# Swin window attention, forward and backward: turning P and dS of a quad by a DMA transpose instead of on TensorE

## The chip, the cores and the metric

The kernel runs on one core of one Trainium2 chip. The metric is the device time of one execution in microseconds. Seven executions of the kernel before took 2029.27 us in the median (2012.38 to 2056.46). The profiled execution took 2029.27 us itself; its span in the profile is 2027.5 us.

## The reference

Attention within windows of 8 x 8 tokens over an image of 256 x 256 tokens of 384 channels, and the gradients of the loss with respect to x and to both weights:

```
xw  = x in windows of 64 tokens              # 1024 windows
qkv = xw @ wqkv                              # q, k, v: 384 channels each
p   = softmax(q k^T * 384 ** -0.5)           # 64 x 64 in each window
out = (p v) @ wo, back in image order
out_1, out_2, out_3 = gradients of x, wqkv, wo for grad_out
```

Everything comes in and goes out in bfloat16.

## The kernel before, in words

The weights are multiplied with each other once at the start (A, B and their transposes), so that per window only products of x and of the gradient with 384 x 384 matrices are left. Two windows, one above the other in the image, make a tile of 128 token rows; four such tiles make a quad. There are 128 quads. `load` brings x (`xq`, from SP's queue) and the incoming gradient (`dq`, from POOL's queue) of a quad, four transfers each. `load_turn` transposes both by DMA on SP's queue, twelve blocks of 128 x 128 each (`dT`, `xT`).

The main loop is a software pipeline over quads, written by hand (L312 to L348 and L363 to L371): in one step, quad C (the oldest) has the second half of its attention products, quad B its scores, softmax and the first half of its attention products, quad A its projections. Ahead of the step, SP issues the transposes for the quad after A, and then the four x loads for the one after that. On POOL, the gradient loads stand between the stores of two steps. The instructions of each engine run in the order in which the program writes them; a step is, on TensorE:

- `scores` of B (tile `sd`), then `uv` of B (eight products of x with B and A^T), with B's softmax on VectorE and ScalarE beside them (`soft`, steps 0 to 5)
- `project(A, 0)`: the gradient's projections (`dT`), evicted by ScalarE to `yz`
- one group of the weight gradient's sums (`filler`, tile `pg`)
- `attend(C, (2, 3))`: the attention products of C's tiles 2 and 3, and after them `turn(B)`
- `project(A, 1)`: x's projections (`xT`) to `yz`; then `to_tokens` has SP transpose `yz` to `tok`, 24 blocks
- one more group of the weight gradient's sums
- `attend(B, (0, 1))`: the attention products of B's tiles 0 and 1

What `turn` works on: `ps` holds, for each tile of a quad and each of its two windows (index w), the softmax P and the score gradient dS stacked over the 128 partitions, 64 columns wide. P is written by ScalarE (L206), dS by VectorE (L218), in `soft` steps 3 and 5. `turn` makes the transposes of these blocks: eight products of `ps` with an identity matrix (L234) into a PSUM tile `pt` from the ring of eight, one VectorE copy (L237) to `PS` in bfloat16. `attend` reads `PS` through `turned` as the weights of its products into `pu`, `po` and `pd` (L256), and `ps` itself in `token_part` (L260). The results go through ScalarE (L265) to `sb` and out by POOL's stores (L246), and through VectorE to `Uq` and `Wq`.

Of the kernel before, what the change touches and what calls it, by code (L numbers as in the profile page):

```python
# [9 lines left out]
ALU = mybir.AluOpType  # L10
AX = mybir.AxisListType
BF16 = mybir.dt.bfloat16
F32 = mybir.dt.float32

P = 128
WIN = 8
WT = WIN * WIN
# [5 lines left out]
def kernel(  # L23
# [88 lines left out]
    def load(st):  # L112
        bp, t0 = st["at"]
        st["xq"] = xq = grp.tile([P, QUAD, C], BF16, tag="xq", name="xq", bufs=2 * GQ + 4)
        st["dq"] = dq = qp.tile([P, QUAD, C], BF16, tag="dq", name="dq", bufs=6)
        for t in range(QUAD):
            nc.sync.dma_start(out=xq[:, t, :], in_=dram_tile(x, bp, t0 + t))
            nc.gpsimd.dma_start(out=dq[:, t, :], in_=dram_tile(grad_out, bp, t0 + t))  # L118
# [62 lines left out]
    def soft(st, step):  # L181
        sd = st["sd"]
        if step == 0:
            st["mx"] = mx = sm.tile([P, QUAD], F32, tag="mx", name="mx")
            for w, h in ((0, HI), (1, LO)):
                nc.vector.tensor_reduce(out=mx[h, :], in_=sd[h, :, w, :], axis=AX.X, op=ALU.max)
        elif step == 1:
            mx = st["mx"]
            st["sh"] = sh = sm.tile([P, QUAD, WT], F32, tag="sh", name="sh")
            for w, h, o in ((0, HI, LO), (1, LO, HI)):  # L190
                nc.vector.tensor_tensor(out=sh[o, :, :], in0=sd[h, :, w, :], in1=over_k(mx[h, :], WT),
                                        op=ALU.subtract)
        elif step == 2:
            st["ex"] = ex = sm.tile([P, QUAD, WT], F32, tag="ex", name="ex")
            nc.scalar.activation(out=ex[:], in_=st["sh"][:], func=ACT.Exp)
        elif step == 3:
            ex = st["ex"]
            rs = sm.tile([P, QUAD], F32, tag="rs")
            nc.vector.tensor_reduce(out=rs[:], in_=ex[:], axis=AX.X, op=ALU.add)
            ri = sm.tile([P, QUAD], F32, tag="ri")  # L200
            nc.vector.reciprocal(out=ri[:], in_=rs[:])
            st["Pb"] = Pb = qp.tile([P, QUAD, WT], BF16, tag="Pb", name="Pb")
            nc.vector.tensor_tensor(out=Pb[:], in0=ex[:], in1=over_k(ri[:]), op=ALU.mult)  # L203
            st["ps"] = ps = qp.tile([P, 2, QUAD, WT], BF16, tag="ps", name="ps")
            for w, h in ((0, LO), (1, HI)):
                nc.scalar.copy(out=ps[h, w, :, :], in_=Pb[h, :, :])  # L206
        elif step == 4:
            st["pr"] = pr = sm.tile([P, QUAD, WT], F32, tag="pr", name="pr")
            for w, h in ((0, LO), (1, HI)):
                nc.vector.tensor_tensor(out=pr[h, :, :], in0=sd[h, :, w, :], in1=st["Pb"][h, :, :], op=ALU.mult)  # L210
            st["D"] = D = sm.tile([P, QUAD], F32, tag="D", name="D")
            nc.vector.tensor_reduce(out=D[:], in_=pr[:], axis=AX.X, op=ALU.add)
        else:
            pd = sm.tile([P, QUAD, WT], F32, tag="pd")
            nc.vector.tensor_tensor(out=pd[:], in0=st["Pb"][:], in1=over_k(st["D"][:]), op=ALU.mult)
            ps = st["ps"]
            for w, h, o in ((0, LO, HI), (1, HI, LO)):
                nc.vector.tensor_tensor(out=ps[o, w, :, :], in0=st["pr"][h, :, :], in1=pd[h, :, :], op=ALU.subtract)  # L218

    def uv(st, t, part):  # L220
        if t == 0 and part == 0:
# [6 lines left out]
        cp(out=dst[:, t, :], in_=pj[:])  # L228

    def turn(st):  # L230
        pt = ring.tile([P, QUAD, 2, WT], F32, tag="r", name="pt")
        for t in range(QUAD):
            for w, h in ((0, LO), (1, HI)):
                nc.tensor.matmul(pt[h, t, :, :].rearrange("p s k -> p (s k)"), lhsT=st["ps"][:, w, t, :],  # L234
                                 rhs=ident[:], start=True, stop=True)
        st["PS"] = dst = qp.tile([P, QUAD, 2, WT], BF16, tag="PS", name="PS")
        nc.vector.tensor_copy(out=dst[:], in_=pt[:])  # L237

    def turned(st, n, t, h):
        if n in ("PT", "ST"):  # L240
# [4 lines left out]
        for h, w in ((LO, 1), (HI, 0)):  # L245
            nc.gpsimd.dma_start(out=dram_tile(dst, bp, t)[WIN * w:WIN * (w + 1)], in_=src[h, :])  # L246

    def attend(st, pair, after=None):
        bp, t0 = st["at"]
        if pair[0] == 0:  # L250
            st["Uq"] = grp.tile([P, QUAD, C], BF16, tag="Uq", name="Uq")
            st["Wq"] = grp.tile([P, QUAD, C], BF16, tag="Wq", name="Wq")
        def both(straight, crossed):
            for h, o, (dst, lhs, rhs, begin, done) in ((LO, LO, straight), (LO, HI, crossed), (HI, LO, crossed),
                                                       (HI, HI, straight)):
                nc.tensor.matmul(dst[o, :], lhsT=turned(st, lhs, t, h), rhs=st[rhs][h, t, :], start=begin, stop=done)  # L256

        def token_part(t, pd, first):
            for w, o in ((0, HI), (1, LO)):
                nc.tensor.matmul(pd[o, :], lhsT=st["ps"][:, w, t, :], rhs=st["tok"][:, :, t, w, :], start=first,  # L260
                                 stop=not first)

        def keep(name, eng, dst, t, src):
            sb = ob.tile([P, C], BF16, tag=name)
            ENG[EV[eng][t]](out=sb[:], in_=src[:])  # L265
            stores.append((dst, sb, bp, t0 + t))

        stores = []
        for t in pair:
            first = t == pair[0]  # L270
            po, pu = [ring.tile([P, C], F32, tag="r", name=n) for n in ("po", "pu")]
            if first:
                pd = ring.tile([P, C], F32, tag="r", name="pd")
                token_part(t, pd, True)
            both((pu, "ST", "xq", True, True), (po, "PT", "uq", True, True))
            keep("o", "o", out_0, t, po)
            ENG[EV["U"][t]](out=st["Uq"][:, t, :], in_=pu[:])  # L277
            pw = ring.tile([P, C], F32, tag="r", name="pw")
            if not first:
                pd = ring.tile([P, C], F32, tag="r", name="pd")  # L280
            both((pw, "Pb", "dq", True, True), (pd, "ST", "vq", not first, first))
            ENG[EV["W"][t]](out=st["Wq"][:, t, :], in_=pw[:])  # L282
            if not first:
                token_part(t, pd, False)
            keep("d", "d", out_1, t, pd)
        for s in stores:
            store(*s)
        if after is not None:
            turn(after)

    fill = []

# [11 lines left out]
    def filler(n):  # L304
        while n and fill:
            try:
                next(fill[0])
                n -= 1
            except StopIteration:
                fill.pop(0)  # L310

    def step(c, b, a):  # L312


        def on(st):
            return (lambda f, *r: f(st, *r)) if st is not None else (lambda f, *r: None)
        C_, B, A = on(c), on(b), on(a)
        B(scores)
        B(soft, 0)
        B(uv, 0, 0)  # L320
        B(uv, 0, 1)
        B(soft, 1)
        B(uv, 1, 0)
        B(uv, 1, 1)
        B(soft, 2)
        B(soft, 3)
        B(uv, 2, 0)
        B(uv, 2, 1)
        for t in range(QUAD):
            A(grad_turn, t)  # L330
        B(uv, 3, 0)
        B(uv, 3, 1)
        B(soft, 4)
        for mo in range(CK):
            A(project, 0, mo)
        B(soft, 5)
        filler(1)
        if c is not None:
            attend(c, (2, 3), b)
        else:  # L340
            B(turn)
        split[0] = True
        for mo in range(CK):
            A(project, 1, mo)
        A(to_tokens)
        filler(1)
        split[0] = ALL
        B(attend, (0, 1))  # L348
# [7 lines left out]
    with tc.manual_schedule(engines=MANUAL):  # L356
        for i in range(min(AHEAD, n)):
            load(sts[i])
            if i < AHEAD - 1:
                load_turn(sts[i])  # L360
        held = []
        get = lambda i: sts[i] if 0 <= i < n else None
        for i in range(-1, n + 1):  # L363
            if AHEAD - 1 <= i + AHEAD - 1 < n:
                load_turn(sts[i + AHEAD - 1])
            if AHEAD <= i + AHEAD < n:
                load(sts[i + AHEAD])
            step(get(i - 1), get(i), get(i + 1))
            if i > 0:
                held.append(sts[i - 1])  # L370
                sts[i - 1] = None  # L371
            if held and (len(held) == GQ or i == n):
                fill.append(gf_group(held))
                held = []
        split[0] = False
        filler(1 << 30)
# [60 lines left out]
```

## Time and profile before

| What | Value |
|---|---|
| Median of seven runs | 2029.27 us (2012.38 to 2056.46) |
| Profiled execution: own time, span | 2029.27 us, 2027.5 us |
| Granted TensorE clock | 0.999 |
| TensorE busy | 1995.4 us, 98% |
| VectorE, ScalarE, POOL busy | 1396.9, 1441.7, 1418.4 us |
| One step of the loop in mid-run (`sd` to `sd`) | 15.38 us |
| L234, `turn`'s products | 1024 of 219 ns |
| L237, `turn`'s copy | 128 of 677 ns |
| dT, xT, tok: issue on SP, median | 2.24, 2.80, 5.06 us |
| dT, xT, tok: issue to landing, median | 6.0, 6.5, 9.4 us |

Busy times are of one execution. Matmuls overlap in TensorE's pipeline, so that the durations of single products add up to more than the time they hold. SP's "duration" of a DMA is the time that SP needs to issue it; its landing comes later, and other engines wait for the landing. The DMA shares count the time that packets are under way on 16 engines; packets of different queues overlap, so that shares can add up to over 100%.

### The profile page before, as it was taken

How to read it: one execution, taken by the hardware profiler on the slowest of the kernel's cores; microseconds unless marked ns; L12 is line 12 of the kernel's file. 1: busy time of each engine (PE TensorE's matmuls, PEld its weight loads, DVE VectorE, ACT ScalarE, POOL GpSimd, SP SyncE). 2: the span in 40 equal slices, each digit the busy share in tenths (PEclk: the TensorE clock that was granted, in tenths of full speed). 3: DMA queues.
4: the chain of work that ended last, by engine and by line, in shares of the span. 5: the costliest groups of instructions: out<-in, count | busy, mean ns of one | idle time of the engine just before them, and what ended most of it. 6: DMA issues, size and time to landing. Idle time of an engine off the chain costs nothing.

```text
span 2027.5 us, 54709 instructions
## 1 busy us (share of the span) xinstructions
PE 1995.4 (98%) x20442; PEld 1222.4 (60%) x20442; DVE 1396.9 (69%) x3107; ACT 1441.7 (71%) x3213; POOL 1418.4 (70%) x2566
## 2 busy tenths in 40 slices
PE   8999999999999999999999999999999999999998
PEld 4565566555566666666666666666666666666665
DVE  5766676666676677677677767767767776776775
ACT  5776777666677777777777777777777777777773
POOL 4766776766777777777776777777777677777764
PEclk9999999999999999999999999999999999999999
DMA  9999999999999999999999999999999999999993
GB/s 212 221 210 204 203 196 207 195 194 187 199 209 206 211 205 209 203 206 208 207 208 206 212 197 214 203 209 209 205 210 203 202 212 208 206 204 210 202 185 79
DMA packets 997195, 409.27 MB, mean 202 GB/s; under 512 B 880705, under 2 KB 971585, under 8 KB 996929
## 3 DMA queue, kind: packets, MB, share of 16 engines
q1 hardware_dynamic: 873648, 253.80, 76.5%
q0 software_dynamic: 122880, 151.68, 30.6%
q8 instruction: 160, 2.62, 0.6%
q14 instruction: 107, 0.87, 0.1%
q10 hardware_dynamic: 400, 0.29, 0.0%
HBM read 101.84 MB, written 101.84 MB: 100 GB/s over the span
## 4 chain that ended last, share of the span: by engine, by line
PE 89%; DMA 5%; ACT 2%; POOL 2%; issue 1%; DVE 1%; ACTq 0%; POOLq 0%
PE pj L146 33%; PE pg L146 12%; PE pj L144 11%; PE pg L144 11%; PE pd L260 6%; PE pu L256 5%; PE sd L146 5%; PE pw L256 4%; DMA out_dram<-sb 3%; PE pt L234 2%; DMA tok<-yz 1%; POOL out_dram L246 1%; DMA dq<-in_grad_out_dram 1%; PE pd L256 1%; ACT uq L228 0%
## 5 line engine op out<-in xcount | busy, mean ns | idle before, releaser
L246 POOL DMA_DIRECT2D out_dram<-sb x2048 | 1145.7, 567 | 539.6 <-ACT sb L265 198.2
L265 ACT CAST sb<-po 128x384 bf16<-128x384 f32 x512 | 250.7, 490 | 289.0 <-PE pu L256 160.3
L301 DVE TENSOR_TENSOR GF_acc<-pg,GF_acc 128x384 f32<-128x384 f32 x258 | 143.9, 558 | 430.4 <-PE pg L144 292.1
L146 PEld LDWEIGHTS <-xT 128*128 128x128 bf16 x3072 | 292.2, 98 | 189.1 <-issue 7.8
L146 PE MATMUL pj<-AT_sb,xT 128*128 128x384 bf16 x1536 | 334.2, 327 | 5.4 <-ACT sb L265 5.2
L146 PE MATMUL pj<-B_sb,xT 128*128 128x384 bf16 x1536 | 333.9, 326 | 0.0
L118 POOL DMA_DIRECT2D dq<-in_grad_out_dram x512 | 273.8, 548 | 49.0 <-issue 14.1
L277 DVE CAST Uq<-pu 128x384 bf16<-128x384 f32 x512 | 282.7, 552 | 18.9 <-PE pu L256 12.1
L228 ACT CAST uq<-pj 128x384 bf16<-128x384 f32 x512 | 248.1, 485 | 56.5 <-PE pj L146 52.4
L282 DVE CAST Wq<-pw 128x384 bf16<-128x384 f32 x512 | 279.8, 547 | 0.0
L265 ACT CAST sb<-pd 128x384 bf16<-128x384 f32 x512 | 254.2, 496 | 35.1 <-DMA out_dram<-sb 28.9
L144 PE MATMUL pj<-xT,A_sb 128*64 128x512 bf16 x2304 | 273.4, 379 | 0.0
L146 PE MATMUL pj<-dT,BT_sb 128*128 128x512 bf16 x1152 | 269.5, 379 | 0.0
L228 ACT CAST vq<-pj 128x384 bf16<-128x384 f32 x512 | 250.5, 489 | 1.9
L144 PEld LDWEIGHTS <-xq 128*64 128x64 bf16 x3000 | 209.2, 110 | 47.5
L162 ACT CAST yz<-pj 128x512 bf16<-128x512 f32 x384 | 222.6, 590 | 14.1 <-PE pj L144 0.2
L146 PEld LDWEIGHTS <-xq 128*128 128x128 bf16 x1572 | 153.1, 98 | 117.7 <-DVE pr L210 4.3
L206 ACT COPY ps<-Pb 64x256 bf16<-64x256 bf16 x256 | 103.2, 403 | 149.6 <-DVE Pb L203 148.1
L160 ACT CAST yz<-pj 128x512 bf16<-128x512 f32 x384 | 206.0, 640 | 0.3 <-PE pj L146 0.2
L144 PEld LDWEIGHTS <-A_sb 128*64 128x64 bf16 x2304 | 149.9, 110 | 68.9 <-issue 0.4
L146 PEld LDWEIGHTS <-BT_sb 128*128 128x128 bf16 x1152 | 112.8, 98 | 122.4 <-issue 0.2
L260 PE MATMUL pd<-tok,ps 128*64 128x384 bf16 x1024 | 181.2, 344 | 3.6 <-DMA tok<-yz 3.6
(63 smaller groups left out, 2672.6 us busy)
## 6 DMA issues: line engine op xcount, KB each, us to landing
out_dram<-sb POOLq DMA_DIRECT2D x2048, 48.0 KB, 4.7
xq<-in_x_dram SPq DMA_DIRECT2D x512, 96.0 KB, 4.4
dq<-in_grad_out_dram POOLq DMA_DIRECT2D x512, 96.0 KB, 4.5
dT<-dq SPq DMA_TRANSPOSE x128, 6.0
xT<-xq SPq DMA_TRANSPOSE x128, 6.5
tok<-yz SPq DMA_TRANSPOSE x128, 9.4
w_sb<-in_wqkv_dram SPq DMA_DIRECT2D x1, 864.0 KB, 5.6
out_dram<-dw_sb SPq DMA_DIRECT2D x1, 864.0 KB, 3.8
```

The costliest lines, as they stand in the source:

```text
L118: nc.gpsimd.dma_start(out=dq[:, t, :], in_=dram_tile(grad_out, bp, t0 + t))
L144: nc.tensor.matmul(out[h], lhsT=lhsT[:, h], rhs=rhs, start=start, stop=stop)
L146: nc.tensor.matmul(out, lhsT=lhsT, rhs=rhs, start=start, stop=stop)
L160: ENG[EV["z"][mo]](out=yz[:, mo, :, 0:4:3, :], in_=pj[:])
L162: ENG[EV["y"][mo]](out=yz[:, mo, :, 1:3, :], in_=pj[:])
L228: cp(out=dst[:, t, :], in_=pj[:])
L246: nc.gpsimd.dma_start(out=dram_tile(dst, bp, t)[WIN * w:WIN * (w + 1)], in_=src[h, :])
L256: nc.tensor.matmul(dst[o, :], lhsT=turned(st, lhs, t, h), rhs=st[rhs][h, t, :], start=begin, stop=done)
L260: nc.tensor.matmul(pd[o, :], lhsT=st["ps"][:, w, t, :], rhs=st["tok"][:, :, t, w, :], start=first, stop=not first)
L265: ENG[EV[eng][t]](out=sb[:], in_=src[:])
L277: ENG[EV["U"][t]](out=st["Uq"][:, t, :], in_=pu[:])
L282: ENG[EV["W"][t]](out=st["Wq"][:, t, :], in_=pw[:])
```

## The change

`turn` becomes one DMA transpose of four 128 x 128 blocks, from `ps` to `PS` in SBUF, on SP's queue. For this, `ps` is laid out tile by tile (the two windows of a tile side by side, so that a tile's block is 128 columns in one piece). The products, the PSUM tile and the VectorE copy go. `turn(B)` is called right after `soft` step 5, ahead of the group of weight gradient sums and of `attend(C, (2, 3))`. The loads for the quad three further on, which stood ahead of the step, now come right after `turn(B)`: on SP the order is the transposes dT and xT, the new transpose, the four x loads, tok.

```diff
-            st["ps"] = ps = qp.tile([P, 2, QUAD, WT], BF16, tag="ps", name="ps")
+            st["ps"] = ps = qp.tile([P, QUAD, 2, WT], BF16, tag="ps", name="ps")
             for w, h in ((0, LO), (1, HI)):
-                nc.scalar.copy(out=ps[h, w, :, :], in_=Pb[h, :, :])
+                nc.scalar.copy(out=ps[h, :, w, :], in_=Pb[h, :, :])
...
             for w, h, o in ((0, LO, HI), (1, HI, LO)):
-                nc.vector.tensor_tensor(out=ps[o, w, :, :], in0=st["pr"][h, :, :], in1=pd[h, :, :], op=ALU.subtract)
+                nc.vector.tensor_tensor(out=ps[o, :, w, :], in0=st["pr"][h, :, :], in1=pd[h, :, :], op=ALU.subtract)
...
     def turn(st):
-        pt = ring.tile([P, QUAD, 2, WT], F32, tag="r", name="pt")
-        for t in range(QUAD):
-            for w, h in ((0, LO), (1, HI)):
-                nc.tensor.matmul(pt[h, t, :, :].rearrange("p s k -> p (s k)"), lhsT=st["ps"][:, w, t, :],
-                                 rhs=ident[:], start=True, stop=True)
         st["PS"] = dst = qp.tile([P, QUAD, 2, WT], BF16, tag="PS", name="PS")
-        nc.vector.tensor_copy(out=dst[:], in_=pt[:])
+        nc.sync.dma_start_transpose(out=dst[:].rearrange("p t s k -> p t (s k)"),
+                                    in_=st["ps"][:].rearrange("p t w k -> p (t w k)"))
...
-    def attend(st, pair, after=None):
+    def attend(st, pair):
...
-                nc.tensor.matmul(pd[o, :], lhsT=st["ps"][:, w, t, :], rhs=st["tok"][:, :, t, w, :], start=first,
+                nc.tensor.matmul(pd[o, :], lhsT=st["ps"][:, t, w, :], rhs=st["tok"][:, :, t, w, :], start=first,
                                  stop=not first)
...
-        if after is not None:
-            turn(after)
...
-    def step(c, b, a):
+    def step(c, b, a, ahead):
...
         B(soft, 5)
+        B(turn)
+        if ahead is not None:
+            load(ahead)
         filler(1)
-        if c is not None:
-            attend(c, (2, 3), b)
-        else:
-            B(turn)
+        C_(attend, (2, 3))
...
-            if AHEAD <= i + AHEAD < n:
-                load(sts[i + AHEAD])
-            step(get(i - 1), get(i), get(i + 1))
+            step(get(i - 1), get(i), get(i + 1), get(i + AHEAD) if i >= 0 else None)
```

## The prediction

> **What bounds the kernel now.** I read the page first: busy shares, the row of DMA shares, the DMA queues, the chain that ended last.
>
> ```profile
> PE 1995.4 (98%) x20442; PEld 1222.4 (60%) x20442; DVE 1396.9 (69%) x3107; ACT 1441.7 (71%) x3213; POOL 1418.4 (70%) x2566
> ...
> DMA  9999999999999999999999999999999999999993
> ...
> q1 hardware_dynamic: 873648, 253.80, 76.5%
> q0 software_dynamic: 122880, 151.68, 30.6%
> ...
> PE 89%; DMA 5%; ACT 2%; POOL 2%; issue 1%; DVE 1%; ACTq 0%; POOLq 0%
> ```
>
> TensorE is busy 98% and carries 89% of the chain. But the DMA queues are close behind: SP's queue (q1, all transposes and the x loads) and POOL's (q0) together have packets under way for more than the time of 16 engines. The DMA row of nines says only that something is always under way, not that nothing more fits. Next, the chain in order of time in the middle of the run:
>
> ```profile
> 999.95 0.86 PE sd L146 x24
> ...
> 1009.95 0.26 PE pt L234 x8
> 1010.21 1.94 PE pj L144 x18
> ...
> 1015.38 0.81 PE sd L146 x24
> ...
> 1030.76 0.81 PE sd L146 x24
> ```
>
> A step of the loop, from one `sd` to the next, is 15.38 us (1015.38 to 1030.76), and TensorE is on the path throughout. The eight products of `turn` (L234) hold 0.26 us of it. They are eight products of 219 ns that overlap. Then the timeline, for what the new transfer has to meet:
>
> ```profile
> 1005.11 2.33 SPq L127 DMA_TRANSPOSE xT<-xq  x1
> ...
> 1006.69 0.85 DVE L218 TENSOR_TENSOR ps<-pr,pd 64x256 bf16<-64x256 f32 x2
> ...
> 1007.49 3.13 SPq L117 DMA_DIRECT2D xq<-in_x_dram  x4
> ...
> 1012.80 5.19 SPq L166 DMA_TRANSPOSE tok<-yz  x1
> ...
> 1014.19 0.35 PE L256 MATMUL pu<-xq,PS 64*64 64x384 bf16 x1
> ```
>
> `ps` is whole at 1007.54; SP is done with issuing xT at 1007.44; the first reader of `PS` starts at 1014.19. Last, the answer on tile xT, its issues (min/median/max in ns) and its landings (from the start of the issue, us), and the SP timeline of an earlier stretch:
>
> ```profile
> L127 SPq DMA_TRANSPOSE xT<-xq x128: 1415/2795/3963, 11.0 to 1958.9; - x128
> ...
> DMA to landing us min/median/max: 3.7/6.5/10.1
> ```
>
> ```profile
> 400.77 7.05 SPq L166 DMA_TRANSPOSE tok<-yz  x1
> 407.99 1.50 SPq L127 DMA_TRANSPOSE dT<-dq  x1
> ...
> 428.02 2.64 SPq L127 DMA_TRANSPOSE xT<-xq  x1
> ...
> 434.16 5.04 SPq L166 DMA_TRANSPOSE tok<-yz  x1
> ```
>
> The issue of twelve blocks takes 1.4 us when the queue has room, and twice that in the median: SP is held back by its queue. And the steps were not all 15.38 us: in that stretch two steps, from `tok` to `tok`, took 33.4 us.
>
> [...] 0.26 us for a quad's four blocks on TensorE, 5.06 us (median) for the issue of `tok`'s 24 blocks, so 0.21 us each. [...]
>
> **The change part by part.**
>
> *Removed from TensorE:* eight products and their weight loads, 0.26 us on the path, 128 times: 33.3 us, 1.6% of 2027.5. That is the whole direct gain.
>
> *Removed from DVE:* the copy L237, 128 x 0.677 = 86.7 us. The chain's 1% for DVE shows no share for it, and between its end (1011.80) and its reader (1014.19) lie 2.4 us. Worth nothing. A PSUM buffer of eight comes free with it; TensorE waits for a buffer almost nowhere in the steady stretch: nothing again.
>
> *The new layout of `ps`:* same instructions, same element counts, inner runs of 64 elements as before: nothing.
>
> *Added on SP:* 128 transposes of four blocks. A block costs 0.12 us (1.41/12, room in the queue) to 0.24 us (2.80/12); so 0.5 to 0.95 us, I take 0.85. SP's step is now 5.06 (tok) + 2.24 (dT) + 2.80 (xT) + 4 x 0.60 to 0.69 (x loads) + 0.5 (gaps) = 13.0 to 13.4; it becomes some 14.2, of 15.12 that TensorE would need (15.38 - 0.26). It fits, but the slack falls from about 2 us to 0.9 us.
>
> *Added on the DMA engines:* four blocks to 48. q1 without x loads is some 67 points of its 76.5 (estimate: the x loads take 9.6, from their packets), so 5.6 points more.
>
> *The new wait and what is queued behind it:* the transpose waits on SP for L218 (and for ACT's L206, earlier). Behind it are the four x loads, then tok, then the next dT. In the timeline SP comes free 0.1 us before `ps` is whole, so the wait is 0.1 to 0.3 us; the x loads go out about 1 us later. A load lands 4.7 us after its issue in the median, the last by about 1016.3 (1007.5 + 1 + 3.1 + 4.7, counted late) and the next dT and xT issues follow at 1018.16: covered. On POOL the gradient loads keep their place between the stores; nothing is moved past them.
>
> *The new deadline:* `PS` must land before the pu product. xT lands 3.7 us after its issue ends; four blocks more at 0.24 are 0.95; so `PS` is there about 4.65 us after SP's release at 1007.5, at 1012.2. It is wanted at 1014.19 - 0.26 = 1013.9. Margin 1.7 us in the median. But xT's landing spreads: going through the transposes of the second half one by one, the 95th percentile of tok's issue to xT's landing is 2.3 us above its median, and the margin is exceeded in about one step of six, by some 0.7 us. Cost: 128/6 x 0.7 = 15 us. Bounds: nothing, if the queue drains while SP waits; 0.26 us a step and more (33 us), if the landing takes a microsecond longer.
>
> *The start:* at 42.75 the xT issue takes 3.85 us and ends at 46.60, while the reader of `PS` runs at 45.95. `PS` would land near 51.3: TensorE is pushed back by 5 us, once, and by 2 us more while SP, running back to back, catches up. 7 us; between 3 and 12.
>
> *Late stretches:* there too SP ends xT (430.66) only 1 us before the reader (431.63). Such lag cost nothing by itself, since only later steps use xT; now each entry into it is a stall of up to 4 us. I put 5 us on this, between 0 and 40.
>
> **Sum for the likeliest case:** 2027.5 - 33.3 + 15 + 7 + 5 = 2021.2; with what lies around the span (this execution is the median run, 2029.27, 1.8 us over its span) 2023. Own range 2003 to 2044.
>
> **The rivals.**
>
> *All of it is hidden.* For it: the margin of 1.7 us, and SP's 0.9 us of slack. Then 2029.3 - 33.3 + 4 for the start = 2000; range 1992 to 2008. Against: the spread of the landings.
>
> *SP's queue becomes the bound (slower).* Place: SP issuing back to back, its queue full. Price: in the late stretch (383.39 to 551.31, ten steps between tok issues) a step lasts 16.8 us, although SP issues nearly without pause. With 0.85 us more for SP and a transfer that TensorE needs in the same step, the kernel may not get out of such stretches, which end by themselves today. It decides from the point at which SP's own step exceeds 15.12 us, 0.9 us above the 14.2 worked out: longer landings of stores or gradient loads are enough. At 15.8 us a step: 128 x (15.8 - 15.38) = 54 more than now, plus the start, 2085; range 2050 to 2130.
>
> *The change doesn't do what it says:* excluded for the products, as the instruction order of the changed kernel has none at L234 and one transpose of 128x4x128 ahead of each quad's x loads.
>
> **How the numbers follow.** About 1% is what a measurement of this kernel can tell from no change. Likeliest case 0.44, all hidden 0.27, queue-bound 0.29. Faster by over 1% (under 2009): all of the hidden case and 0.05 of the likeliest, 0.32. Slower by over 1% (over 2049.6): the queue-bound case nearly whole, 0.28. Within: 0.40. The range leaves out the lower half of the hidden case's and the upper third of the queue-bound one's: 1997 to 2085.
>
> **What would show it.** Right: `sd` to `sd` 15.1 us in most steps, no L234, waits of the PE weight load of `PS` for a DMA `PS<-ps` in a sixth of the steps, up to 2 us; `PS` landing 5 to 6 us after its issue begins; SP's waits ahead of tok down to below 1 us. All hidden: hardly any such wait. Queue-bound: a step over 15.5 us throughout, SP back to back, and the DMA share of the chain well over 5%. The prediction would be wrong if stores land later for the added packets and hold ACT's L265 longer than the 86.5 us it now waits for them.

## The result, and the profile after

| What | Before | After |
|---|---|---|
| Median | 2014.17 us (62 executions, 2009.86 to 2086.55) | 2030.40 us (25 executions, 2022.20 to 2041.51) |
| Ratio to before | 1 | 1.0067, 95% interval 1.0047 to 1.0087 |
| Profiled execution: own time, span | 2029.27 us, 2027.5 us | 2043.39 us, 2041.6 us |

The changed kernel is slower by 0.7% in this ratio, which leaves out executions of over 1.5% above the fastest of their kernel; the medians of all executions differ by 16 us. How the kernel before scatters came out only with more executions than the seven shown at first: half of them take 2010 to 2015 us, 27 of the 62 take over 2020 us, up to 2086, and the profiled one is of these. The profiled execution of the kernel after is slower than all of its 25 others, so that its waits are those of a bad case.

The page of the kernel after has these rows: busy time of the engines, the two DMA queues, the shares of the chain that ended last, and the group of the first products that read `PS` (busy us, mean ns of one | idle before it, and what ended the idle time):

```profile
PE 1971.7 (97%) x19418; PEld 1195.1 (59%) x19418; DVE 1323.5 (65%) x2979; ACT 1426.6 (70%) x3213; POOL 1419.5 (70%) x2566
...
q1 hardware_dynamic: 943280, 270.60, 79.9%
q0 software_dynamic: 122880, 151.68, 32.7%
...
PE 78%; DMA 18%; ACT 2%; POOL 1%; issue 1%; DVE 0%; SPq 0%; POOLq 0%; ACTq 0%
...
L252 PE MATMUL pu<-xq,PS 64*64 64x384 bf16 x1024 | 176.5, 337 | 52.7 <-DMA PS<-ps 51.1
```

TensorE lost 23.7 us of busy time (1995.4 to 1971.7), as its 1024 products are gone; 33.3 us had been forecast, and where the rest stayed is shown below. Its share of the chain fell from 89% to 78%, and DMA's rose from 5% to 18%. The last row names the DMA: the product that reads `PS` first was held up for 51.1 us by the landing of the new transpose. SP's queue has its packets under way for 79.9% instead of 76.5%, and POOL's 32.7% instead of 30.6%, although POOL moves the same bytes as before.

The view of waits of the kernel after counts them (us in total, times, longest):

```profile
PEld L252 <- DMA PS<-ps: 75.4, 62, 4.9
PE pu L252 <- DMA PS<-ps: 51.1, 43, 4.5
```

43 of 128 steps have a stall of the products, of 1.19 us on average (51.1 / 43), which is 0.40 us a step. The change took 0.26 us a step off TensorE. The weight loads' 75.4 us overlap these and are not added.

A long stall can cost more than its own length. One of them in TensorE's timeline, with the group of `sd` just after it and the same group in another step:

```profile
661.14 0.35 PE L252 MATMUL pu<-xq,PS 64*64 64x384 bf16 x1 [2.24 <-DMA PS<-ps]
...
662.71 1.46 PE L146 MATMUL sd<-xT,yz 128*128 128x64 bf16 x24
...
1005.62 0.87 PE L146 MATMUL sd<-xT,yz 128*128 128x64 bf16 x24
```

The view of windows has for the 3.4 us behind the stall (stretch, its length, busy time and number of products, granted clock, busy share of the DMA engines, GB/s):

```profile
661.50:664.90 3.40, 3.40 (x42) 0.50 1.15 254
```

TensorE was granted half its clock there, and the same 24 products took 1.46 us instead of 0.87. Leaving out the last 45 us (the end behind the loop), the kernel after has seven such stretches, 27.3 us in all, each during or within 1.5 us behind a wait for `PS` of 1.7 to 4.5 us; the kernel before has one of 3.4 us, at a wait of 3.2 us. Neither profile has one without such a wait, though not every long wait has one: behind six others for `PS`, of 1.7 to 2.5 us, the kernel after has none. The mean granted clock is 0.993 instead of 0.999. The two spans then differ by these terms: 33.3 us of products are gone, 9.6 us of busy time came back (33.3 - 23.7), most likely by the lower clock, and TensorE's idle time grew by 37.8 us (from 32.1 to 69.9, spans less busy time). 2027.5 - 33.3 + 9.6 + 37.8 is 2041.6.

Tile `PS` of the kernel after (issue on SP in ns, minimum, median, maximum; then the landing, in us from the start of the issue):

```profile
L232 SPq DMA_TRANSPOSE PS<-ps x128: 1188/1240/2505, 33.2 to 2006.3; - x128
...
DMA to landing us min/median/max: 2.4/5.3/8.2
```

Never is the issue shorter than 1.188 us, for four blocks. Last, the chain in order of time around a step that stalls, and from the timeline of the same stretch SP's issues and VectorE's last write to `ps`:

```profile
1005.69 0.81 PE sd L146 x24
...
1013.65 6.87 DMA PS<-ps
...
1020.56 0.35 PE pu L252
...
1021.69 0.81 PE sd L146 x24
```

```profile
1003.11 5.79 SPq L166 DMA_TRANSPOSE tok<-yz  x1
1009.08 2.29 SPq L127 DMA_TRANSPOSE dT<-dq  x1
1011.55 1.99 SPq L127 DMA_TRANSPOSE xT<-xq  x1
1012.37 0.85 DVE L218 TENSOR_TENSOR ps<-pr,pd 64x256 bf16<-64x256 f32 x2
...
1013.65 1.60 SPq L232 DMA_TRANSPOSE PS<-ps  x1
...
1015.30 3.43 SPq L117 DMA_DIRECT2D xq<-in_x_dram  x4
1018.83 4.99 SPq L166 DMA_TRANSPOSE tok<-yz  x1
```

The step lasts 16.0 us (1005.69 to 1021.69). In it SP goes from one issue to the next with gaps of at most 0.2 us: the wait for `yz` ahead of `tok`, 2 us in the kernel before, is gone. `ps` is whole at 1013.22, SP comes to the new transpose only at 1013.65, and the products get `PS` 6.87 us later. Added up over the middle of the run (300 to 1800 us, from the same view), SP's issues and the gaps between them are, per step:

| Kernel | Issues | Gap ahead of tok | Other gaps |
|---|---|---|---|
| before (48 blocks) | 13.08 us | 1.71 us | 0.77 us |
| after (52 blocks) | 14.40 us | 0.42 us | 0.68 us |

Some 0.6 us of gaps stay where SP never waits (five of 0.05 to 0.18 us). SP thus needs about 15.0 us (14.40 + 0.6), and a step that TensorE sets has 15.12 us.

### The profile page after: what moved, and what is told of

The parts are those of the page before. It is cut to its first block, busy times and chain, and to the rows that moved or that the text cites. A ratio compares the mean times of both kernels' runs of the same rounds, so it can differ in the third digit from the quotient of the medians.

```text
span 2041.6 us, 53125 instructions
## 1 busy us (share of the span) xinstructions
PE 1971.7 (97%) x19418; PEld 1195.1 (59%) x19418; DVE 1323.5 (65%) x2979; ACT 1426.6 (70%) x3213; POOL 1419.5 (70%) x2566
## 3 DMA queue, kind: packets, MB, share of 16 engines
q1 hardware_dynamic: 943280, 270.60, 79.9%
q0 software_dynamic: 122880, 151.68, 32.7%
## 4 chain that ended last, share of the span: by engine, by line
PE 78%; DMA 18%; ACT 2%; POOL 1%; issue 1%; DVE 0%; SPq 0%; POOLq 0%; ACTq 0%
PE pj L146 35%; DMA PS<-ps 15%; PE pg L146 10%; PE pj L144 8%; PE pg L144 7%; PE sd L146 5%; PE pu L252 5%; PE pd L256 5%; PE pw L252 3%; DMA out_dram<-sb 2%; ACT yz L160 1%; POOL out_dram L242 1%; DMA dq<-in_grad_out_dram 0%; PE pd L252 0%; DMA xT<-xq 0%
## 5 line engine op out<-in xcount | busy, mean ns | idle before, releaser
L252 PE MATMUL pu<-xq,PS 64*64 64x384 bf16 x1024 | 176.5, 337 | 52.7 <-DMA PS<-ps 51.1
L206 ACT COPY ps<-Pb 64x256 bf16<-64x256 bf16 x256 | 103.2, 403 | 149.6 <-DVE Pb L203 148.1
L144 PEld LDWEIGHTS <-A_sb 128*64 128x64 bf16 x2304 | 156.3, 109 | 78.2 <-DMA xT<-xq 1.2
L252 PEld LDWEIGHTS <-PS 64*64 64x64 bf16 x3072 | 112.5, 106 | 140.5 <-DMA PS<-ps 75.4
```

The lines of the kernel that those rows point to most:

```text
L144: nc.tensor.matmul(out[h], lhsT=lhsT[:, h], rhs=rhs, start=start, stop=stop)
```

## The experiments

Two theories. The *deadline*: `PS` lands too late for its reader, but SP and the DMA engines can carry it. The *load*: with 52 blocks and their issues SP's queue is full, whoever reads what and when. The executions of the kernel before scatter, so that the median of those measured beside an experiment differs from one to the next (2011.87 to 2036.93). Where a kernel has only four to six executions, its own median is compared, and small differences are not clear.

**Take the deadline away, or take the reader away.** The first kernel lets tiles 0 and 1 read the `PS` of the quad before:

```diff
-            return st["PS"][h, t, int((n == "ST") == (h == LO)), :]
+            return st["use"][h, t, int((n == "ST") == (h == LO)), :]
...
-    def attend(st, pair):
+    def attend(st, pair, older=None):
...
+        st["use"] = (older or st)["PS"]
...
-        B(attend, (0, 1))
+        B(attend, (0, 1), c)
```

> The changed kernel, but tiles 0 and 1 of a quad are attended with the PS of the quad before (the older P and dS, so these two tiles of each quad are computed from other data); every instruction and transfer stays, only the deadline of the new transfer goes from the same step to the next. Theory 1, the landing of PS in its own step is what eats the gain: no wait for PS, steps of 15.1 us, the kernel before minus 25 to 33 us (ratio 0.984 to 0.988). Theory 2, the load of four more blocks on SP and its queue slows the rest: still at or over the kernel before (ratio 1.00 to 1.01).

Measured: 2029.63 us (20 executions), 1.0052 (1.0022 to 1.0083). The view of waits:

```profile
ACT sb L262 <- DMA out_dram<-sb: 128.0, 174, 2.4
...
PE pu L253 <- DMA PS<-ps: 3.8, 1, 3.8
```

The waits for `PS` are gone but for one, and in the median not a microsecond came back. SP issues for 14.60 us a step here and has 0.11 us ahead of `tok`; it lags, and ScalarE now waits for the stores (128.0 us; 14.9 in the kernel after, 86.5 in the kernel before). The profiled execution, 2017.09 us, is one of the faster ones of this kernel, so that its waits say what is gone, but not where all of the median's time went. The deadline by itself is not the cause.

The second has TensorE make `PS` as before, and in the new place SP does the same transpose into a buffer that nobody reads:

```diff
     def turn(st):
...
+        nc.sync.dma_start_transpose(out=spare[:].rearrange("p m c -> p (m c)")[:, 0:QUAD * P].rearrange(
+            "p (t k) -> p t k", t=QUAD), in_=st["ps"][:].rearrange("p t w k -> p (t w k)"))
...
         C_(attend, (2, 3))
+        B(turn_pe)
```

> The kernel before with TensorE's turn and the VectorE copy kept and read, plus the new transpose at its new place with the x loads behind it, into a tile that nobody reads. Theory 1: the load by itself costs little, ratio 1.000 to 1.005. Theory 2: the load is the cost, ratio 1.02 to 1.03 (the 16 us by which the changed kernel is slower, and the 33 us that TensorE does not save here).

Measured: 2050.19 us (4), 1.0141 (1.006 to 1.0221). This lies between the two expectations. A transfer that nobody reads comes with 36 us over the median of before, and its four executions lie close together (2049.31 to 2051.03). SP issues for 14.63 us a step and has only the fixed gap of 0.11 us ahead of `tok`. No deadline is left in this kernel; what it has more than the kernel before is the load.

**Only the move of the x loads**, in the kernel before:

```diff
         B(soft, 5)
+        if ahead is not None:
+            load(ahead)
...
-            if AHEAD <= i + AHEAD < n:
-                load(sts[i + AHEAD])
```

> The kernel before with only the x and gradient loads moved behind soft step 5, its turn left on TensorE and no new transpose. SP does not wait for the softmax here, so nothing should change: ratio 0.997 to 1.003. If the move were what fills SP's queue: 1.005 to 1.014.

Measured: 2013.46 us (20), 0.998 (0.9943 to 1.0017). No cost of the move shows.

**Order, and half of it.** The turn goes ahead of xT on SP:

```diff
         B(turn)
+        if turns is not None:
+            load_turn(turns, "x")
...
-                load_turn(sts[i + AHEAD - 1])
+                load_turn(sts[i + AHEAD - 1], "d")
```

> The changed kernel with the new transpose ahead of xT's on SP (dT, PS, xT, x loads, tok), so that it no longer lies behind twelve blocks. Theory 1: PS lands about 3 us earlier, next to no waits for it, ratio to the kernel before 0.984 to 0.990. Theory 2: as the changed kernel or slower, 1.005 to 1.02, since xT, the x loads and tok go out 1 to 2 us later.

Measured: 2031.91 us (20), 1.0087 (1.006 to 1.0113). No better than the kernel after. `PS` lands 4.8 us after the start of its issue in the median (5.3 in the kernel after); the waits of the products for `PS` fell from 51.1 to 33.8 us, and ScalarE's for the stores rose to 57.2.

Next, tiles 0 and 1 are turned on TensorE and only 2 and 3 by DMA:

```diff
-                                    in_=st["ps"][:].rearrange("p t w k -> p (t w k)"))
+                                    in_=st["ps"][:, 2:].rearrange("p t w k -> p (t w k)"))
...
         C_(attend, (2, 3))
+        B(turn_pe, (0, 1), "PE")
```

> Tiles 0 and 1 turned by TensorE and VectorE as in the kernel before, tiles 2 and 3 (needed one step later) by a DMA transpose of two blocks at the changed kernel's place. Theory 1: half of TensorE's saving, none of the wait, 12 to 17 us faster than before, ratio 0.991 to 0.994. Theory 2: no gain, ratio 1.00 to 1.01. By the way, the issue of two blocks tells whether SP's time for a small transpose goes with its blocks (0.6 us) or has a floor (1.2 us as with four).

Measured: 2026.54 us (20), 1.0036 (1.0006 to 1.0066). The issue of two blocks took 1.170 us at least and 1.526 in the median, as long as that of four, and SP issues for 14.64 us a step. Two blocks fewer do not relieve SP. The 4 us gained over the kernel after come with half of the products back on TensorE (64 times 0.26, some 17 us), so the blocks themselves seem to count for something too; the difference is small beside the scatter of both kernels.

**Four blocks fewer elsewhere.** `tok` has 20 blocks in place of 24, so that SP is back at 48 with the change in. Tiles 2 and 3 multiply the tokens of tiles 0 and 1.

```diff
-        nc.sync.dma_start_transpose(out=tok[:].rearrange("p m t b k -> p (m t b) k"),
-                                    in_=st["yz"][:].rearrange("p m t s k -> p (m t s k)"))
+        nc.sync.dma_start_transpose(out=tok[:].rearrange("p m t b k -> p (m t b) k")[:, 0:20],
+                                    in_=st["yz"][:].rearrange("p m t s k -> p (m t s k)")[:, 0:20 * P])
...
-                nc.tensor.matmul(pd[o, :], lhsT=st["ps"][:, t, w, :], rhs=st["tok"][:, :, t, w, :], start=first,
+                nc.tensor.matmul(pd[o, :], lhsT=st["ps"][:, t, w, :], rhs=st["tok"][:, :, t % 2, w, :], start=first,
```

> The changed kernel with four blocks taken off tok's transpose (20 of 24), so that SP transposes 48 blocks a quad as in the kernel before; tiles 2 and 3 multiply the tokens of tiles 0 and 1, with the same products. Theory 2 (SP's queue is full with 52 blocks): most of the loss goes, 1985 to 2003 us, what is left being waits for PS of 0.1 to 0.2 us a step. Theory 1 (the landing alone): no better than the changed kernel, 2025 to 2032.

Measured: 1999.42 us (4), 0.9907 (0.9838 to 0.9975): 31 us less than the kernel after. Its waits:

```profile
PE pu L252 <- DMA PS<-ps: 17.1, 15, 4.0
```

The waits for `PS` fall to a third. SP issues for 13.37 us a step and waits 0.93 us ahead of `tok` again.

With 48 blocks, the deadline was taken away once more, by the older `PS` (both edits from above together):

> The same 48 blocks, and besides tiles 0 and 1 attended with the PS of the quad before, so that neither the fuller queue nor the deadline is left. Both theories: TensorE's whole saving, 1978 to 1988 us. If it stays over 2000, something else than these two costs time, as the move of the x loads.

Measured: 1987.40 us (4), 0.9845 (0.9775 to 0.9915). And with 48 blocks and the turn ahead of xT:

> The changed kernel with 48 blocks (tok of 20; tiles 2 and 3 multiply the tokens of tiles 0 and 1) and the new transpose ahead of xT's. With room in SP's queue the order should count: 1984 to 1993 us, near the 1987 of the version that reads the older PS. If the order does not help even then, 1997 to 2005 us as with 48 blocks and the changed kernel's order.

Measured: 1989.55 us (4), 0.9822 (0.9726 to 0.9918). The page's chain, and the waits:

```profile
PE 97%; DMA 1%; ACT 1%; DVE 0%; issue 0%; ACTq 0%
```

```profile
PE pu L257 <- DMA PS<-ps: 8.3, 4, 3.3
```

So with room on SP the deadline is worth 10 to 12 us, and order alone gets them back; with SP full the same two edits brought nothing. The landing, from the start of the issue, is 4.2 us in the median ahead of xT and 5.1 behind it.

The kernel before with 20 blocks of `tok` (44 in all) shows whether before was at that edge already:

> The kernel before with four blocks fewer in tok (20 of 24; tiles 2 and 3 multiply the tokens of tiles 0 and 1), 44 blocks a quad. If the kernel before is itself at the edge of SP's queue, its slower executions (up to 2090 us) go and every execution lies at 2008 to 2014 us. If those have another cause, they stay.

Measured: 2009.00 us (20, 2007.36 to 2013.44), 0.9951 (0.9924 to 0.9977). Measured beside it, 39 executions of the kernel before spread from 2010.03 to 2061.56. The gain over its usual time is small, but the tail is gone: the late stretches of before hang on the number of blocks too. With the change in and four blocks more (48, turn ahead of xT), the time is lower by 2009.0 - 1989.6 = 19 us.

**SP's time, or the blocks?** Two small copies (128 rows of two elements) on SP, unread, instead of the transpose, with the turn on TensorE:

```diff
+        for k in range(2):
+            nc.sync.dma_start(out=spare[:, 0, 16 * k:16 * k + 2], in_=st["ps"][:, k, 0, 0:2])
...
+        B(turn_pe)
```

> The kernel before's turn on TensorE kept, and at the place of the new transpose two small copies of 128 x 2 elements on SP into a tile that nobody reads, x loads behind them: SP's time (about 1.2 us, as long as the new transpose takes to issue) without its 512 rows of packets. If SP's time counts: as with the unread transpose, 2040 to 2052 us. If the packets count: 2011 to 2025 us.

Measured: 2029.97 us (4), 1.005 (0.9981 to 1.012). Between the two expectations, and not clear of no change. SP issues for 14.69 us a step, as much as with the unread transpose (14.63), also without a wait, and no block is added. The four executions lie 16 us over the median of before, those with the transpose 36 us. That suggests that issue time on SP brings a part and the blocks another, but with four executions each it does not show it. Nor are the copies free of packets, as the expectation has it: by the pages they add 36,864 to SP's queue (873,648 to 910,512), the unread transpose 69,632 (to 943,280). The same two copies behind the new transpose, in the kernel with 48 blocks:

```diff
+        for k in range(2):
+            nc.sync.dma_start(out=spare[:, 0, 16 * k:16 * k + 2], in_=st["ps"][:, k, 0, 0:2])
```

> The changed kernel with 48 blocks (tok of 20; tiles 2 and 3 multiply the tokens of tiles 0 and 1) and two small copies of 128 x 2 elements on SP after the new transpose: the blocks of the kernel before, but 1.2 us more of SP's time a step, as much as four blocks and more. If SP's own time is what was full with 52 blocks: back to 2020 to 2045 us. If the blocks on the DMA engines were: 1998 to 2010 us, as with 48 blocks alone.

Measured: 2077.33 us (4), 1.0269 (1.0145 to 1.0394), 78 us over the same kernel without the copies. Its waits:

```profile
PE pu L255 <- DMA PS<-ps: 84.2, 61, 3.8
```

SP issues for 14.97 us a step (each copy 0.59 us in the median); with the fixed gaps this is over the 15.12 us of TensorE. How late SP comes can be read from the traces (300 to 1900 us): from the end of the last write to `ps` to the start of the transpose's issue it is 0.07 us in the median with 48 blocks, 0.57 in the kernel after and 1.17 here, and the products wait 17.1, 51.1 and 84.2 us for `PS`. From the start of its issue the transpose lands after 5.1, 5.4 and 5.1 us, nearly alike. So a late SP is enough to bring the loss, and more than it, without one block added. The copies' packets come with it, but the packets of SP's queue are under way for no larger share than without the copies (77.9% against 79.4%). Of the 78 us some 17 are TensorE's clock: 41.0 us at half of it, instead of 6.8 (mean granted clock 0.990 and 0.998).

**Relieving SP of issues, with 52 blocks.** All x loads go out from ScalarE's queue:

```diff
-            nc.sync.dma_start(out=xq[:, t, :], in_=dram_tile(x, bp, t0 + t))
+            nc.scalar.dma_start(out=xq[:, t, :], in_=dram_tile(x, bp, t0 + t))
```

> The changed kernel with the x loads issued by ScalarE's queue in place of SP's: SP's step loses some 2.7 us, the blocks and bytes are the same; ScalarE gets 4 x 0.6 us. If SP's own time is what is full: 1985 to 2010 us, SP with waits again. If the drain of the transposes on the DMA engines is what is full: SP's issues get longer instead, tok 6 us and more, and the time stays at 2025 to 2045.

Measured: 2116.65 us (4), 1.0505 (1.041 to 1.06). A miss:

```profile
ACT sb L261 <- issue: 220.4, 96, 4.2
```

ScalarE itself was held up, so this says nothing about SP. Two of four loads on ScalarE, at a place where it waits for the softmax, with the turn ahead of xT:

```diff
         B(soft, 2)
+        if ahead is not None:
+            load_half(ahead)
         B(soft, 3)
```

> The whole computation. The changed kernel with the new transpose ahead of xT's, and two of a quad's four x loads issued by ScalarE's queue between soft steps 2 and 3, where ScalarE waits 1.16 us for VectorE in every step. SP's step loses 1.2 us, back under TensorE's 15.12. If SP's own time is what is full: 1986 to 2005 us, faster than both kernels (ratio 0.982 to 0.995). If the 52 blocks fill the DMA engines whatever SP does: 2020 to 2035 us, with longer issues of tok. If ScalarE is held up by the two issues: over 2035.

Measured: 2104.21 us (6), 1.0435 (1.0401 to 1.047), a second miss. The waits of SP's queue:

```profile
SPq L139 <- DMA dq<-in_grad_out_dram: 185.6, 57, 6.6
```

SP, with fewer loads to issue, stands ahead of dT for the gradient (1.80 us a step in its timeline, 0.20 in the kernel after), and everything behind dT stands with it: the products wait 72.1 us for `PS`.

A quad's x as one transfer of 128x1536 instead of four; the tokens stand in another order for it:

```diff
+        quad = x[0, 2 * WIN * bp:2 * WIN * (bp + 1), WIN * t0:WIN * (t0 + QUAD), :]
+        nc.sync.dma_start(out=xq[:].rearrange("p t c -> p (t c)"), in_=quad.rearrange("r (q s) c -> r q (s c)", q=WIN))
         for t in range(QUAD):
-            nc.sync.dma_start(out=xq[:, t, :], in_=dram_tile(x, bp, t0 + t))
```

> The changed kernel, 52 blocks, with a quad's x loaded by one transfer of 128 runs of 1536 elements (tokens stand in another order, so the windows mix; the work is the same) in place of four of 128 runs of 384: SP's step loses about 2 us, the bytes stay, and no other engine gets anything to do. If SP's own time is full: 1983 to 2003 us. If the blocks on the DMA engines are: 2018 to 2032 us, with tok's issue grown to 6 us and more.

Measured: 2073.32 us (4), 1.02 (1.0053 to 1.0348), although SP issues for only 12.78 us a step and waits 1.87 us ahead of `tok`. Either `PS` was late for its place behind dT and xT, or the engines cannot carry 52 blocks. Two more kernels ask this: this load with the older `PS`, and this load with the turn ahead of xT (the edits shown above).

> The changed kernel with all 52 blocks, a quad's x loaded as one transfer of 128x1536 (the tokens of a quad stand in another order, so that windows mix tokens of a row) and tiles 0 and 1 multiplied by the PS of the quad before: SP is relieved by some 2 us a step and PS has no deadline in its own step. If the gradient loads' late stretches reach TensorE only through PS, which stands behind dT and xT on SP: 1985 to 2000 us, a median step of 15.12 us and hardly a wait for PS. If 52 blocks are more than the DMA engines take, whatever SP issues: 2015 us or more, with the waits moved to tok, to dT or to the stores.

> The changed kernel with all 52 blocks, a quad's x loaded as one transfer of 128x1536 (the tokens of a quad in another order, as in the run beside it) and the turn of P and dS issued ahead of xT but still behind dT. If the order on SP is what made PS late when SP had room: 2000 to 2030 us, the waits for PS halved against the 157 us of the kernel with the turn behind xT. If it is dT's wait for the gradient loads that holds the turn back: 2050 to 2075 us, with the waits for PS about as large as there.

Measured: 2300.30 us (4), 1.137 (1.1288 to 1.1453), and 2324.57 us (4), 1.1495 (1.1413 to 1.1577). The second is far over both of its expectations. By the first one's time, and by its waits for dT and the stores, the engines would be the limit, as its second expectation has it. But the waits of this kernel say something else. The waits of the kernel with the older `PS`:

```profile
ACT sb L263 <- DMA out_dram<-sb: 393.0, 286, 5.6
POOL out_dram L243 <- DMA dq<-in_grad_out_dram: 253.9, 124, 6.7
```

and from its page:

```profile
DMA packets 1011521, 425.89 MB, mean 188 GB/s; under 512 B 944192, under 2 KB 969536, under 8 KB 1011264
...
dq<-in_grad_out_dram POOLq DMA_DIRECT2D x512, 96.0 KB, 5.5
```

The engines moved the bytes of the kernel after in a longer time, at 188 GB/s, less than the 209 of that kernel. What was late were the gradient loads (landing 5.5 us in the median, 4.6 in the kernel after), for which POOL stood 124 times (34 times in the kernel after, 28.0 us), and SP ahead of dT (3.29 us a step in its timeline; 0.20 in the kernel after). TensorE then stalled often enough to be at half its clock for 136.5 us (27.3 in the kernel after; mean granted clock 0.970 and 0.993). The larger x load brought a wait on POOL that neither theory had. So these three kernels do not test the relief of SP alone, and whether 52 blocks go through with SP relieved stays open.

**Three blocks fewer, with nothing left out.** The kernel has a switch that turns the gradient's first tile of a quad on TensorE, with a VectorE copy to `dT`. With it, SP has 49 blocks:

```diff
-    G_ON_PE = 0
+    G_ON_PE = 1
```

> The changed kernel, the whole computation, with the gradient's first tile of every quad turned by three transposes on TensorE and a VectorE copy, so that SP has 49 blocks a step. TensorE gets back some 0.2 us a step (three blocks against the four of the products taken away, 0.26 us), 26 us in all, on top of the 1999 us with 48 blocks: if SP's queue with 52 blocks is the cause, 2015 to 2028 us, SP waiting again and PS waits near the 60 us of the run with 48 blocks; if 52 blocks are not the cause, 2045 us or more, the waits of the changed kernel plus the added products.

Measured: 2070.04 us (5), 1.0238 (1.0169 to 1.0307). The waits, and the chain in order of time:

```profile
PEld L146 <- DVE dT L136: 85.6, 127, 0.8
...
PE pj L146 <- DVE dT L136: 37.2, 128, 0.4
...
PE pu L252 <- DMA PS<-ps: 8.9, 5, 3.5
```

```profile
1015.33 0.81 PE sd L146 x24
...
1020.08 0.36 DVE dT L136
1020.49 2.12 PE pj L146 x9
...
1031.11 0.81 PE sd L146 x24
```

The time expected under the load theory was missed by 42 us, but not for the reason of the other theory: the waits for `PS` are nearly gone (8.9 us), SP waits 1.42 us ahead of `tok`, and the step is 15.78 us nearly throughout. In its place TensorE waits in every step for the new copy (its weight loads 0.67 us, 85.6 / 127, and its products 0.29 us, 37.2 / 128, at the same time), which stands on VectorE behind the softmax and just ahead of the projections that read it. The longer step gives SP room too, so that this kernel does not separate the three blocks from the longer step.

With the turn ahead of xT as well:

> The same with the turn of P and dS issued ahead of xT, the whole computation. 1990 us with 48 blocks and this order, plus the three transposes' 26 us: 2008 to 2020 us, hardly a wait for PS, and level with the kernel before. If the order costs again what it costs with 52 blocks: as the run beside it, or 2030 us.

Measured: 2066.02 us (5), 1.0225 (1.0145 to 1.0305). The same waits for the copy, 85.6 and 37.2 us, and waits of the products for `PS` of 4.0 us. Without them 2066 would be 1980 at best, by the weight loads, or 2029, by the products; that is only worked out. Turning the tile earlier, between `soft` steps 1 and 3, where VectorE waits for ScalarE, was not tried. None of the kernels that leave nothing out was measurably faster than the kernel before.

## Why the prediction was wrong

The forecast was 2023 us, somewhat faster; it became 2030.4, slower than before. The time lies in the range, the sign is wrong.

- *The 33.3 us off TensorE* were right: steps without a wait last 15.15 us with 48 blocks (15.12 expected), and with SP relieved of four blocks the kernel falls to 1987 to 1990 us.
- *The copy on VectorE, the freed PSUM buffer, the new layout, the x loads' move: nothing.* For the move no cost was measured (2013.46 against 2019.76 of the kernel before beside it). No wait of the profile after shows the others, and the writes of `ps` take 404 ns (L206) and 420 ns (L218) in the median with either layout.
- *"Added on SP ... I take 0.85": this step failed.* The price was made by the block, from 0.12 to 0.24 us, out of issues of twelve blocks (1.41 us at the shortest, 2.80 in the median); that SP's queue makes the difference between the two was the author's estimate. But a transpose of four blocks takes 1.19 us at least to issue, 1.24 in the median and 1.44 in the mean, beyond the upper bound of 0.95. With `tok` held back more (5.33 us in the median, 5.06 before), SP's issues grew by 1.32 us a step (13.08 to 14.40). The step of SP became not 14.2 but about 15.0 us: nearly nothing was left of the 0.9 us of slack.
- *"PS lands 4.65 us after SP's release ... margin 1.7 us"* failed in part as a consequence, in part by itself. That the new blocks land behind xT's was the author's estimate, from xT's landing alone. With room on SP `PS` landed 5.0 us (49 blocks) and 5.1 us (48 blocks) after the start of its issue, half a microsecond later than the sum has it, though in the range of 5 to 6 us that the prediction itself named as a sign of being right. With SP full, SP comes to the transpose late and the landing takes 5.3 us: a stall in 43 steps of 128 instead of one in six, of 1.19 us instead of 0.7. That is 51.1 us instead of 15 + 7 + 5.
- *"The start ... 7 us; between 3 and 12"* was too low. The sixth `sd` comes at 89.2 us in the kernel before and at 101.9 after; with the 1.3 us that five steps should have saved, the start cost 14 us. TensorE waited for `PS` there not once but four times, 11.7 us in the first 100 us.
- *What a stall costs* was put at its own length, and what follows it at nothing. With half the clock at the long ones (27.3 us of it, which is at most some 14 us of work) TensorE's busy time kept 9.6 of the 33.3 us, most likely for this. Between the two profiled executions this is nearly half of the difference to the forecast: 2041.6 against 2021.2 is 20.4 us, of which 9.6 are this and 10.8 are idle time (37.8 instead of 27).
- *The late stretches at 5 us, with the profiled execution as the base.* The base itself was in the tail. The kernel before takes 2010 to 2015 us in half of its executions, and with four blocks fewer in all of them 2007 to 2013 us. The range of the seven, 2012.38 to 2056.46, was a sign that something was at its edge already.
- *"5.6 points more" on SP's queue* became 3.4 (76.5% to 79.9%). The x loads' 9.6 points were low: alone on ScalarE's queue they take 12.8%.
- *The rival "SP's queue becomes the bound"* had place and mechanism right, and its point of decision (an SP step of 15.12 us). It was too dear: the step did not rise to 15.8, since SP stands just at the edge and not over it. Of its signs the DMA share well over 5% of the chain is there (18%), the step of over 15.5 us throughout is not (15.16 us in the median).
- *"Stores land later and hold ACT's L265 longer"* was named as what would make the forecast wrong. ScalarE waits less for stores in the kernel after (14.9 us), most likely since TensorE waits for `PS` first; where the deadline is gone, that wait comes back (128.0 us).

Not settled is how the load divides between SP's issue time and the DMA engines. That a late SP brings a loss of this size and more is shown by the copies in the kernel with 48 blocks (78 us), which add few bytes (0.15 MB) but also packets (36,864). That relieving SP would undo the loss with 52 blocks is not shown, as each way of relieving it (x loads on ScalarE, all or half; one larger x load) brought a new wait.

## What to carry to other kernels

A saving on the busiest engine counts only if the queue that takes over the work has room, and the room has to be added up queue by queue, issue times and gaps, against the step that the busiest engine would then need (here 14.40 and 0.6 us against 15.12). A short transfer is priced by its own shortest issue (here 1.19 us for four blocks), not by the share of a long one (0.85). Where the executions of a kernel scatter upwards, a queue may be at its edge already: here four blocks fewer took the tail away (all 20 executions at 2007 to 2013 us), and four more made every execution (2022 to 2042 us) slower than the usual one of before (2010 to 2015). And a stall on the busiest engine is to be priced with the clock that follows it (here half of it, for 3.4 us behind a wait of 2.24 us), not by its length alone.

## What was not expected of the hardware

- The shortest issues of DMA transposes on SP were nearly alike for two blocks and for four, 1.170 and 1.188 us; for twelve it was 1.41 us in the kernel before.
- Two copies of 512 bytes each (128 rows of two elements) on SP cost the kernel with 48 blocks 78 us (1999.42 to 2077.33).
- During or behind seven waits of TensorE of 1.7 to 4.5 us in the kernel after, and one of 3.2 us in the kernel before, its granted clock fell to half for 3.4 us, once for 6.8; at no other place in these two profiles did it, their last 45 us left out.
- One x load of 384 KB in place of four of 96 KB, with the deadline away, came with gradient loads landing at 5.5 us instead of 4.6, and with 2300 us. Some 68 us of that are the clock (136.5 us at half of it); why the loads land later is not shown.
